# Sparse attention into a hard-swish MLP on one core: PSUM regrouped into four double banks, with score, value and GEMM 1 steps made wider

## The chip, the cores and the metric

The kernel runs on one core of a Trainium2 chip. The metric is the device time of one execution in microseconds (us), as the median of several runs; three runs of the kernel before gave 218.65 to 219.04 us with a median of 218.84 us. A core has five engines with a queue each: TensorE (PE, matmuls; its weight loads are listed as PEld), VectorE (DVE), ScalarE (ACT), GpSimd (POOL) and SyncE (SP). Here POOL and SP mostly issue DMAs. Matmuls write to PSUM, which has eight banks of 128 x 512 f32; DVE and ACT move results from PSUM to SBUF.

## The reference

Attention over 4 batches, 8 heads, 768 positions and head size 64, and then an MLP over the 3072 tokens. Each query sees the keys closer than 16 positions, plus 24 summary keys (the maximum of each block of 32 keys, with log 32 added to the score; the value is the mean of the block).

```
k_sum = k.reshape(B, H, nb, 32, D).max(3);  v_sum = v.reshape(B, H, nb, 32, D).mean(3)
scores_l = where(|i - j| < 16, q k^T / 8, -1e9);  scores_s = q k_sum^T / 8 + log(32)
attn = softmax(concat(scores_l, scores_s)) @ concat(v, v_sum)
x = attn.transpose(0, 2, 1, 3).reshape(3072, 512)
h = x @ w_in                                   # 512 -> 2048
out = (h * clip(h + 3, 0, 6) / 6) @ w_out      # 2048 -> 512
```

## The kernel before

**Attention.** A batch is cut into 12 blocks of 64 queries. A block meets 96 keys of its window and the 24 summary keys, so a score tile has 120 rows. Its plan names each step by a letter and numbers. `s` is the score step: matmuls of 64 x 64 for a pair of heads (`scores`, line 641), an `exp` on ACT that writes the tile `at` (line 651), and on DVE a product with a 0/1 mask (line 655). For batch 0 the first half of the queries instead gets its mask through a matmul with a bias (line 629). `u` forms the sums of the values (`vsum`, lines 665 and 682) and copies them into the tile `vaug`. `v` is the value step (`values`, line 742): at x vaug, with a column of ones that gives the softmax denominator, for tokens in tiles `T` of 128; `finish` takes the reciprocal (line 775), normalizes on DVE into `xn` (line 779) and turns it into `x` with tokens along the columns. For batches 0 and 1 the turn is four TensorE transposes (line 797) and a copy; for batches 2 and 3 it is a DMA transpose on SP's queue (line 789), one per `T`. `k`, `q` and `w` prepare transposed keys and queries; batch 0 and 1 do it with TensorE, batch 2 with DVE, batch 3 with DMA transposes (lines 570 and 579).

**The MLP.** A half batch of 384 tokens is a stage `s` (0 to 7). `F` is GEMM 1 (`f1`): for each of 16 blocks of 128 columns of w_in, four matmuls of 384 columns into one bank `h` (line 815), then a Relu on ACT into `r` (line 820) and min-and-multiply on DVE into `g` (line 822). `G` is GEMM 2 (`f2`): for each of the 3 token tiles, 16 matmuls of 512 columns into one bank, in four quarters of four (line 835), a copy to `ot` and a store by SP (lines 846 and 847).

**PSUM before.** Pools: three single banks `h` (GEMM 1), one single bank `o` (GEMM 2) and two double banks `S` (scores, values, transposes).

**Order.** The order of all steps is written out by hand in the long string `ORDER`; `F21.4` is step 4 of stage 2's second group of four column blocks, and a suffix `:A` or `:D` says that ACT or DVE does it. Each engine runs its own steps strictly in that order and waits on semaphores. `Plan.run` only picks buffers and adds a few filler matmuls on the tile `idle` (line 927) while PE waits in the first 23 us. Loads (`K`, `Q`, `V`, `h`, `I` for w_in, `O` for w_out) are issued by POOL in the same way; DMAs of x, keys and queries that transpose, and all stores, by SP.

Of the kernel before, what the change touches and what calls it, by code (L numbers as in the profile page):

```python
# [9 lines left out]
F32 = mybir.dt.float32  # L10
# [19 lines left out]
K01.0 K02.0 c.0 c.9 z1.0:D e.0 f.0 e.3 c.8 e.1 e.2 z0.0:A z2.0:A Q010.0 Q000.0 c.1 k01.0 k01.1 K00.0 k03.0 V00.0 c.2 c.4  # L30
k01.3:A z3.0:A k01.2:A k03.1 k02.0 s030.0 q030.0 q030.1:A q010.0 s010.0 k03.2:A q000.0 V02.0 V01.0 c.6 V03.0 k02.1 k02.3:A
k03.3:A k01.4 q010.1:D k02.4 k03.4 q000.1:D c.7 k02.2:D k00.0 s010.1 q020.0 s030.1 s010.2 q020.1:A s030.2 k00.1 k00.4 e.4
h000.0:D h020.0:D h010.0:D h021.0:D u00.0 s000.0 u00.1:A u00.2:A k00.2:A s020.0 s020.1 u02.0 s020.2 u01.0 s000.1 u01.1:A
s000.2 u02.1:A h011.0:D u01.2:D h030.0:D u03.0 u03.1:D h031.0:D v00.0 v02.0 v00.1 v01.0 v01.1 u01.3:A k00.3:A u02.2:A v00.2
v00.3 v02.2 v01.2 Q01w0.0 Q01w1.0 Q01w2.0 v02.1 v00.4 q021.0 q021.1:A s021.0 s021.1 v01.3 v00.5:D v02.3 v02.4 v02.5 I0.0 I1.0
I2.0 K11.0 c.3 I3.0 Q10.0 K10.0 K13.0 K15.0 K12.0 K14.0 Q13.0 Q14.0 Q11.0 Q15.0 Q12.0 O0.0 O1.0 O2.0 O3.0 h11.0 h10.0 q031.0
q031.1:A v02.6 v01.4 v01.5:A q011.0 q011.1:A u00.3:D v02.7:D u03.2:D c.5 h001.0:D F00.10 s031.0 s031.1 F00.0 F00.1 F00.2
F00.11 F00.12 q001.0 s031.2 F00.3 F00.13 q001.1:A F00.15 F00.16 F00.4 s021.2 F00.14 F00.17 s011.0 F01.0 s001.0 F01.9 F01.6
s011.1 F01.1 s011.2 F01.2 s001.1 s001.2 F01.10 F01.7 F01.11 F01.8 F00.5 F00.6 F00.7 v03.0 v04.0 F02.6 v03.1 v04.1 v03.2 F01.3
v04.2 v05.0 v03.3 F02.7 F00.8 F01.4 v03.4:A F02.8 v05.1 F00.9 v05.2 F01.5 F02.3 F02.4 F02.5 F02.0 v04.3 v05.3 F02.1 F02.2  # L40
v04.4:D v05.4:A F03.9 F03.3 F10.0 F03.10 F03.4 F10.1 F03.11 F03.5 F10.6 F13.9 F10.7 F13.10 F10.2 F10.8 F13.11 F03.6 F12.6
k10.0 F03.7 F03.8 k10.1:D k11.0 F12.7 F12.8 k11.1:D F10.9 k12.0 F10.10 F10.11 F02.9 F02.10 k12.1:A k13.0 F10.3 F03.0 F10.4
F02.11 k13.1:A F03.1 F10.5 F11.9 q11.0 F03.2 F11.10 q11.1:A F11.11 q10.0 F11.0 F11.3 q10.1:A F11.1 q13.0 q13.1:A F11.4 w1.0
F11.2 w1.4:D F11.5 G00.0 q12.0 F12.9 F12.0 F12.3 G00.1 F12.10 q12.1:A F12.1 w1.3:A G00.2 w1.1 w1.2:D s120.0 F12.2 F12.11
F11.6 G00.3 s120.3 s120.1 F13.0 s110.0 F11.7 F13.1 s110.1 s110.3 F12.4 G00.4:D F11.8 V13.0 V12.0 V10.0 V11.0 h12.0 G02.0
G02.1 s100.0 G02.2 G02.3 s100.1 s100.3 s130.0 F13.3 s130.1 s110.4 s110.2 F12.5 s120.4 G02.4:D G01.0 u1.0 G01.1 G01.2 s120.2
s100.2 s100.4 s130.2 F13.2 F13.4 s130.3 u1.1:A u1.4:A u1.8:D u1.6:D u1.2:D u1.7:A u1.5:A v10.0 G01.3 G01.4:A F13.6 u1.3:D
F13.5 v10.5 v10.1 v10.2 v10.6 s130.4 u1.9:D v10.3 v10.4:A F13.7 V21.0 K23.0 K20.0 K22.0 K21.0 V20.0 Q22.0 Q23.0 Q21.0 V23.0
Q20.0 h21.0 h20.0 K35.0 G11.0 G01.5 G02.5 G00.5 v12.0 F13.8 v12.5 v12.1 v12.2 v12.6 G11.1 G11.2 v10.7 v12.3 G11.3 v10.8:D
v12.4:D F20.0 F20.1 v12.7 v12.8:A F21.9 F21.6 F21.10 k21.0 k20.0 F21.7 F20.2 G11.4:D F21.11 F21.8 v14.0 F22.0 F20.9 F23.6  # L50
F20.10 F23.7 F22.1 k22.0 k23.0 F23.8 F22.2 v14.5 G12.0 G12.1 G12.2 F22.6 F22.7 F20.11 w2.0 v14.1 F22.8 v14.2 F21.0 F20.3
G12.3 F20.4 F21.1 F22.3 G12.4:A F22.4 F20.5 F21.2 v14.3 F20.6 F23.0 v14.6 F22.5 q20.0 F23.1 F20.7 v14.4:A w2.4:D F20.8 G10.0
v14.7 v14.8:A F22.9 G10.1 F21.3 F21.4 w2.3:A F22.10 G10.2 G10.3 w2.1 F23.2 F21.5 q22.0 F22.11 q21.0 F33.6 F30.0 G10.4:A F23.9
G20.0 G20.1 q23.0 q24.0:D w2.2:A F30.1 F30.2 F33.7 F33.8 F23.10 s210.0 F23.11 F32.9 F31.0 F23.3 s210.1 s210.3 F32.10 s220.0
s220.1 F31.1 F32.11 G20.2 F33.3 s220.3 F33.4 F23.4 F31.2 F33.5 F23.5 h31.0 V30.0 V32.0 h30.0 K34.0 V33.0 h22.0 V22.0 V31.0
h32.0 Q34.0 K30.0 Q31.0 u2.0 u3.0 u2.1:D u2.8:A u3.1:D u2.6:D F32.6 F30.6 F30.7 F33.9 s230.0 F33.10 u2.9:D F30.8 u2.2:D
F33.11 K32.0 K31.0 Q32.0 K33.0 Q33.0 Q35.0 Q30.0 G10.5 G12.5 k3e0.0 q3x0.0 G11.5 F32.7 s230.1 s230.3 G20.3 F31.6 F30.9 s200.0
G20.4:A u2.4:D s220.4 F32.8 u3.5:D s200.1 s210.2 s230.4 s200.2 s210.4 u2.5:D s220.2 s230.2 G21.0 F31.3 G21.1 G21.2 G21.3
u2.7:A s200.3 F31.7 F30.10 F31.8 F31.4 v20.0 F30.11 u2.3:D v20.1 F31.5 v20.4 G21.4:A v20.5 s200.4 v20.2 F31.9 F30.3 F31.10
F30.4 u3.8:A G22.0 G22.1 v22.0 F33.0 F33.1 G22.2 G22.3 G22.4:A v22.1 v22.4 F31.11 F30.5 F33.2 v22.2 v22.5 F32.3 F32.0 F32.1  # L60
F32.2 v24.0 F32.4 v24.4 F32.5 w3.0 w3.4:D v20.3 k3e1.0 v20.6 v22.3 G22.5 G30.0 G30.1 G30.2 G30.3 F40.0 F41.0 F43.9 G30.4:A
w3.1 F40.1 F41.1 F43.10 w3.2:D F40.2 w3.3:D v24.5 F41.2 u3.6:A F43.11 q3x1.0 G21.5 G30.5 v22.6 G20.5 v24.6 G32.0 G32.1 F40.6
F42.3 G32.2 F42.4 v24.1 v24.2 v24.3 F42.5 u3.9:A F40.7 F40.8 F43.3 F43.4 s320.0 F42.6 F42.0 s320.1 F42.7 s320.3 F42.1 F43.5
u3.7:D s320.2 F42.2 F41.6 F41.7 G32.3 G32.4:A s310.0 F42.8 F40.3 F40.4 u3.2:A F40.5 F50.0 F50.1 G31.0 F50.2 F41.8 u3.4:D
# [43 lines left out]
class Plan:  # L108
# [43 lines left out]

    def run(self):
# [7 lines left out]
        for token in ORDER.split():  # L161
# [8 lines left out]
            for a in o.alloc:  # L170
                a.pool = min((p for p in a.among if self.pools[p]), key=lambda p: min(x for x, _ in self.pools[p]))
                s = min(self.pools[a.pool], key=lambda s: s[0])
                self.pools[a.pool].remove(s)
                a.slot, t = s[1], max(t, s[0])
# [27 lines left out]
            for b in o.bufs:  # L202
                b.left -= 1
                b.used[e] = o.done
                b.end = max(b.end, o.done)
                if b.left == 0:
                    self.pools[b.pool].append((b.end + 0.02, b.slot))
                    self.lives.append((b.begin, b.end, b.slot))
# [761 lines left out]
```

## Time and profile before

| | |
|---|---|
| median of 3 runs | 218.84 us (218.65 to 219.04) |
| profiled execution, its own time | 219.68 us |
| its span in the profile | 217.9 us |
| granted TensorE clock | 0.999 |
| DVE busy | 148.3 us (68%) |
| ACT busy | 122.3 us (56%) |
| POOL busy | 71.2 us (33%) |
| DMA | 24.67 MB at a mean of 113 GB/s |

The profiled execution took 1.8 us more than its span, and 0.8 us more than the median of the runs. Busy time of an engine is not enough to say what bounds the kernel: matmuls are pipelined and their listed durations overlap, so the spacing of their starts, the chain of work that ended last and the waits have to be read beside it. The lines themselves are shown in the prediction.

### The profile page before, as it was taken

What the parts mean: (1) busy time and instruction counts of PE and PEld (TensorE: products, weight loads), DVE (VectorE), ACT (ScalarE), POOL (GpSimd) and SP (SyncE); (2) the same over time, 40 slices, a digit from 0 to 9 for tenths busy, and PEclk for the clock granted to TensorE, in tenths of its full rate; (3) what the DMA queues carried; (4) which work ended last, traced back from release to release, by engine and by line L of the source; (5) the groups of instructions that cost most, each with busy time, mean ns of one, the idle gap of its engine ahead of it and who ended that gap; (6) DMA issues with size and microseconds to landing.
All of it is one profiled execution on the core that took longest, in us unless ns stands there. A gap on an engine that the chain in (4) does not pass through costs nothing.

```text
span 217.9 us, 5201 instructions
## 1 busy us (share of the span) xinstructions
PE 207.1 (95%) x2125; PEld 118.4 (54%) x2151; DVE 148.3 (68%) x304; ACT 122.3 (56%) x236; POOL 71.2 (33%) x90
## 2 busy tenths in 40 slices
PE   7888999999989999989999999999999999999993
PEld 2566666765545555555555555555555555555552
DVE  4878998794898999849987866695555456333301
ACT  5697967797762545777742688833436343423010
POOL 7999369810988466296000000000000000000000
PEclk9999999999999999999999999999999999999999
DMA  5999999999999999999927920005421001201213
GB/s 68 182 156 191 201 164 159 205 195 147 122 120 164 169 122 143 162 172 148 212 52 180 230 26 0 3 0 157 135 48 51 0 2 50 99 0 48 86 59 100
DMA packets 109929, 24.67 MB, mean 113 GB/s; under 512 B 101072, under 2 KB 106960, under 8 KB 109904
## 3 DMA queue, kind: packets, MB, share of 16 engines
q0 software_dynamic: 93440, 14.89, 110.3%
q1 hardware_dynamic: 16464, 9.44, 16.4%
q8 instruction: 17, 0.28, 0.5%
q14 instruction: 8, 0.07, 0.1%
HBM read 29.77 MB, written 6.29 MB: 165 GB/s over the span
## 4 chain that ended last, share of the span: by engine, by line
PE 53%; DMA 25%; POOL 17%; issue 3%; ACT 0%; POOLq 0%; ACTq 0%
PE h L815 23%; PE o L835 22%; DMA vaug<-in_v_dram 20%; DMA win<-in_moe_w_in_dram 5%; PE h L835 5%; POOL nat L434 4%; POOL vaug L445 3%; POOL nat L425 2%; PE S L742 2%; POOL wout L485 1%; PE S L641 1%; POOL qwide L412 1%; POOL win L479 1%; POOL nat L392 1%; POOL nat L399 1%
## 5 line engine op out<-in xcount | busy, mean ns | idle before, releaser
L822 DVE SCALAR_TENSOR_TENSOR g<-r,h 128x384 bf16<-128x384 f32 x128 | 67.8, 547 | 42.6 <-ACT r L820 41.3
L815 PE MATMUL h<-x,win 128*128 128x384 bf16 (+1 forms) x536 | 94.5, 319 | 0.0
L820 ACT ACTIVATE r<-h 128x384 f32<-128x384 f32 x128 | 60.4, 496 | 55.2 <-PE h L815 51.6
L835 PE MATMUL o<-wout,g 128*128 128x512 bf16 x313 | 78.4, 379 | 1.6 <-issue 0.6
L815 PEld LDWEIGHTS <-win 128*128 128x128 bf16 x536 | 49.3, 98 | 34.0 <-issue 0.2
L835 PEld LDWEIGHTS <-g 128*128 128x128 bf16 x400 | 38.2, 98 | 37.2
L651 ACT ACTIVATE at<-S 120x768 bf16<-120x768 f32 x32 | 25.2, 816 | 4.7 <-PE S L641 4.6
L445 POOL DMA_DIRECT2D vaug<-in_v_dram x16 | 15.4, 968 | 4.4 <-DMA wout<-in_moe_w_out_dram 2.3
L655 DVE TENSOR_TENSOR at<-at,mask 96x768 bf16<-96x768 bf16 x28 | 14.7, 550 | 1.7 <-ACT at L651 1.6
L494 ACT COPY ot<-o 128x512 f32<-128x512 f32 x14 | 8.3, 589 | 13.3 <-PE o L835 13.2
L779 DVE TENSOR_TENSOR xn<-S,rc 128x512 bf16<-128x512 f32 x23 | 15.4, 683 | 0.3
L425 POOL DMA_DIRECT2D nat<-in_k_dram x12 | 10.7, 898 | 4.4 <-DMA win<-in_moe_w_in_dram 3.3
L425 POOL DMA_DIRECT2D nat<-in_q_dram x12 | 10.6, 897 | 1.9 <-DMA win<-in_moe_w_in_dram 1.9
L835 PE MATMUL h<-wout,g 128*128 128x256 bf16 (+1 forms) x64 | 10.7, 326 | 0.1
L707 DVE TENSOR_REDUCE red<-kb 128x48 bf16<-128x1536 bf16 x6 | 10.5, 1745 | 0.0
L641 PEld LDWEIGHTS <-kb 64*128 64x128 bf16 x384 | 6.8, 95 | 6.2 <-issue 5.0
L742 PEld LDWEIGHTS <-at 120*64 120x64 bf16 x360 | 6.7, 111 | 4.9 <-issue 2.9
L742 PE MATMUL S<-vaug,at 120*64 120x65 bf16 x352 | 8.0, 197 | 0.9 <-DVE vaug L494 0.9
L494 ACT COPY vaug<-vs 24x768 bf16<-24x768 bf16 x9 | 7.4, 828 | 1.1 <-DVE vs L494 0.9
L494 DVE COPY vaug<-vs 24x768 bf16<-24x768 bf16 x15 | 7.7, 517 | 0.5
L494 ACT COPY ot<-h 128x256 f32<-128x256 f32 (+1 forms) x3 | 1.3, 443 | 11.6 <-PE h L835 11.6
L494 DVE COPY ot<-o 128x512 f32<-128x512 f32 x7 | 4.8, 688 | 4.4 <-PE o L835 2.6
(107 smaller groups left out, 155.8 us busy)
## 6 DMA issues: line engine op xcount, KB each, us to landing
out_dram<-ot SPq DMA_DIRECT2D x19, 256.0 KB, 2.5
vaug<-in_v_dram POOLq DMA_DIRECT2D x16, 192.0 KB, 9.6
win<-in_moe_w_in_dram POOLq DMA_DIRECT2D x4, 512.0 KB, 9.4
wout<-in_moe_w_out_dram POOLq DMA_DIRECT2D x4, 512.0 KB, 10.0
nat<-in_k_dram POOLq DMA_DIRECT2D x12, 128.0 KB, 8.4
nat<-in_q_dram POOLq DMA_DIRECT2D x10, 128.0 KB, 5.4
nat<-in_k_dram POOLq DMA_DIRECT2D x6, 192.0 KB, 6.7
nat<-in_q_dram POOLq DMA_DIRECT2D x6, 192.0 KB, 10.7
```

The source lines that it names most:

```text
L425: nc.gpsimd.dma_start(out=o[n:128], in_=src[b, :, lo + n:lo + 128].rearrange("h r d -> r h d"))
L445: op("POOL", 0.945, lambda: nc.gpsimd.dma_start(out=o[BLK:WIN, lo:hi, 0:D], in_=rows[:, lo:hi]), w=[("v", b % 2, c)], dma=1.28, els=1536)
L494: {"ACT": nc.scalar.copy, "DVE": nc.vector.tensor_copy, "POOL": nc.gpsimd.tensor_copy}[eng](o, i)
L651: op("ACT", 0.81, lambda a=a, x=x: nc.scalar.activation(a, x.slot[0:KEYS, :, 0:HALF], AF.Exp, scale=scl), r=[x], w=[("at", p, half)])
L655: op("DVE", 0.55, lambda m=m, half=half: nc.vector.tensor_tensor(m, m, mask[:, low(half):low(half) + HQ].unsqueeze(1).to_broadcast([WIN, 2 ...
L707: nc.vector.tensor_reduce(red.slot[:].rearrange("x (p u e n) -> x e u p n", p=NP, u=NS, e=2)[:, e], w[:, n * e:n * e + n, BLK:WIN].rearran ...
L742: nc.tensor.matmul(y, a[:, cols], vaug[b % 2][0:KEYS, h, t, 0:D + 1], start=True, stop=True)
L779: nc.vector.tensor_tensor(o, src[..., 0:D], r.unsqueeze(len(r.shape)).to_broadcast(list(o.shape)), op=ALU.mult)
L815: nc.tensor.matmul(h.slot[:, lo * 128:hi * 128], w_in_sb[:, kt, ft * 128:(ft + 1) * 128], xt[s].slot[:, kt, lo * 128:hi * 128], start=(kt ...
L820: op("ACT", 0.49, lambda: nc.scalar.activation(r.slot[:], h.slot[:, 0:HALF], AF.Relu, bias=0.5, scale=1.0 / 6.0), r=[h], w=[r], alloc=r)
L822: op("DVE", 0.553, lambda: nc.vector.scalar_tensor_tensor(gt[s].slot[:, ft], r.slot[:], 1.0, h.slot[:, 0:HALF], op0=ALU.min, op1=ALU.mult) ...
L835: nc.tensor.matmul(o.slot[:, a:z], gt[s].slot[:, ft, ts * 128:(ts + 1) * 128], w_out_sb[:, ft, a:z], start=(ft == 0), stop=(ft == NFT - 1))
```

## The change

PSUM becomes two tiles of four banks. `S` is used as two double banks and `h` as four single banks or as two double banks (`hh`). Steps may take from either.

- **GEMM 1** does two column blocks at once into one double bank: the same matmuls, then one Relu and one min-and-multiply over 2 x 384 columns. `r` has two buffers of twice the size.
- **Scores** of batches 1 to 3: three steps (`scores_all`) of 32 matmuls, each into all four banks of `S`, with one `exp` over 2 x 1024 and one mask product, in place of four steps of 24 matmuls with two of each.
- **Values** of batches 1 to 3, and of the second half of batch 0: one step per half batch (`values_half`) of 48 matmuls into the four banks of `S`, one reciprocal and two normalizations, in place of one step per two tiles `T` (for batch 0: per tile).
- **x** of batches 1, 2 and 3: one DMA transpose per half batch. In batch 1 it takes the place of six groups of four TensorE transposes and their copies. Batch 0 still uses TensorE. `x` has three buffers in place of four.
- The constant tile `ind` is built on DVE, not on POOL; the constants `idle`, `band3`, `bias` and `sums` lie in the third `g` buffer.
- The last GEMM 2 tile is split into columns of 256, 128 and 128, not of 256 and 256.
- `ORDER` is new throughout. In the first stretch, batch 0's query block for the second half (`Q01w`) is loaded ahead of the values, and all of batch 0's scores and values come ahead of the first `F`.

```diff
-        "h": [ps.tile([128, 512], F32, tag=f"h{i}", name=f"h{i}") for i in range(3)],
-        "o": [ps.tile([128, 512], F32, tag="o0", name="o0")],
-        "S": pairs,
-        "x": [sb([128, NP, HALF], BF16, f"x{i}") for i in range(4)],
-        "r": [sb([128, HALF], F32, f"r{i}") for i in range(4)],
+    four = ps.tile([128, 4, 512], F32, tag="S", name="S")
+    banks = ps.tile([128, 4, 512], F32, tag="h", name="h")
+    pairs = [t[:, 2 * i:2 * i + 2] for t in (four, banks) for i in range(2)]
...
+        "h": [banks[:, i] for i in range(4)],
+        "S": pairs[:2],
+        "x": [sb([128, HALF // 128, NP, 128], BF16, f"x{i}") for i in range(3)],
+        "xm": [sb([128, 3 * d_model], BF16, "xm"), qwide[:].rearrange("p u m -> p (u m)")],
+        "r": [sb([128, 2, HALF], F32, f"r{i}") for i in range(2)],
...
+    def scores_all(b, k):
+        X, n = [Buf("S"), Buf("S")], NP * NQ // 3
...                                                   # 32 matmuls into four[:, 2 * j + i // 8, ...]
+        op("ACT", 1.88, lambda: nc.scalar.activation(odds[0:KEYS, :, w], four[0:KEYS].rearrange("p (j e) c -> p j (e c)", j=2), AF.Exp, scale=scl),
+           r=X, w=[("atg", k)])
+        op("DVE", 1.22, lambda: nc.vector.tensor_tensor(...mask..., op=ALU.mult), r=["mask", "masks"], w=[("atg", k)])
...
+    def values_half(b, half):
+        X, xm, rc, s, each = [Buf("S"), Buf("S")], Buf("xm"), Buf("rc"), 2 * b + half, 6
...                                                   # 48 matmuls into four[...]
+        op("DVE", 0.21, lambda: nc.vector.reciprocal(...), r=X, w=[rc], alloc=rc)
+        for g in range(2):
+            op("DVE", 0.97, lambda g=g: nc.vector.tensor_tensor(xm.slot[:, 768 * g:768 * g + 768]..., op=ALU.mult), ...)
+        if b:
+            op("SP", 1.3, lambda: nc.sync.dma_start(out=xt[s].slot[:].rearrange("p u k c -> p (u k) c"), in_=xm.slot[:], transpose=True), ...)
+            return
...                                                   # batch 0: TensorE transposes and copies
     def f1(s, ft):
-        h, r = Buf("h"), Buf("r")
+        h, r = Buf(("hh", "S")), Buf("r")
-        op("ACT", 0.49, lambda: nc.scalar.activation(r.slot[:], h.slot[:, 0:HALF], AF.Relu, bias=0.5, scale=1.0 / 6.0),
+        op("ACT", 0.81, lambda: nc.scalar.activation(r.slot[:], h.slot[:, :, 0:HALF], AF.Relu, bias=0.5, scale=1.0 / 6.0),
-        op("DVE", 0.553, lambda: nc.vector.scalar_tensor_tensor(gt[s].slot[:, ft], r.slot[:], 1.0, h.slot[:, 0:HALF],
+        op("DVE", 0.955, lambda: nc.vector.scalar_tensor_tensor(gt[s].slot[:, ft:ft + 2], r.slot[:], 1.0, h.slot[:, :, 0:HALF],
...
-        for p in range(NP):
-            scores(b, [(p, 0), (p, 1)])
+        for i in range(3):
+            scores_all(b, i)
         vsum(b)
-        for Ts in ((0, 1), (2, 3), (4, 5)):
-            values(b, Ts)
+        for x in range(2):
+            values_half(b, x)
...
-                f2(s, *part, cols=(0, d_model // 2))
-                f2(s, *part, cols=(d_model // 2, d_model))
+                for c in ((0, 256), (256, 384), (384, 512)):
+                    f2(s, *part, cols=c)
```

The parts of the new `ORDER` that the prediction speaks of: the end of the start, the last part of batch 1's attention with GEMM 1 of stages 3 and 2, and the end.

```
... u02.0 u02.1:A u02.2:A h011.0:A u01.3:A ... v00.0 v01.0 v00.1 v01.1 v02.0 v02.1 ... v00.4 v01.3 v03.0 ...
v02.2 v02.3 v00.5:A v01.4 v01.5:D v03.1 v02.4 v03.2 v03.3 F00.0 F00.1 F00.2 ...
... v13.0 v13.1 v13.2 v13.3 G00.5 v13.4 G01.5 G12.0 G02.1 G02.2 v10.0 G12.1 G12.2 G02.3 G12.3 k22.0
v10.1 v10.2 k21.0 v10.3 k23.0 G12.4:A G12.5 G11.5 F30.0 F30.1 F30.4 F30.5 F31.0 F31.1 ... F33.3 v10.4 G02.5 F20.0 ...
... G62.0 G62.1 G62.2 G62.3 G72.4:D G72.5 G71.1 G71.4 G71.7 G71.12 G62.4:A G62.5 G71.13:A G71.14
```

More of the change, by code (lines that the diff above doesn't have):

```diff
@@ L43 @@
[L43 to L52, printed above, removed]
@@ L85 @@
 SLOW = 5.8
+TAKEN = 1e9
 TURN = 0.11
@@ L151, in room, with take, give @@
         return t
+    def take(self, a):
+        best = None
+        for p in a.among:
+            own = self.pools["h" if p == "hh" else p]
+            ts = [max(own[2 * m:2 * m + 2]) for m in range(len(own) // 2)] if p == "hh" else own
+            for n, x in enumerate(ts):
+                if x < TAKEN and (best is None or x < best[0]):
+                    best = x, p, n
+        t, a.pool, n = best
+        a.at = [("h", 2 * n), ("h", 2 * n + 1)] if a.pool == "hh" else [(a.pool, n)]
+        for p, m in a.at:
+            self.pools[p][m] = TAKEN
+        a.slot = self.slots[a.pool][n] if a.pool != "hh" else self.wide[n]
+        return t
+    def give(self, a):
+        for p, m in a.at:
+            self.pools[p][m] = a.end + 0.02
+            self.lives.append((a.begin, a.end, self.slots[p][m]))
     def run(self):
@@ L170, in run @@
             for a in o.alloc:
[L171 to L174, printed above, removed]
+                t = max(t, self.take(a))
             for k in o.bufs:
@@ L276 @@
     qwide = sb([128, NS // 2, d_model], BF16, "qwide")
-    sums = sb([128, NP, 2, D + 2], BF16, "sums")
-    vf = [sums[:, c] for c in range(NP)]
     w_in_sb = sb([128, NP, d_ff], BF16, "win")
@@ L301 @@
     })
+    plan.wide = pairs[2:]
     op = plan.op
@@ L346, in const_ops @@
         op("DVE", 0.64, over=0.0, fn=spread, r=["band", "band3"], w=["mask"])
+        op(EITHER, {"ACT": 0.85, "DVE": 0.45}, lambda eng: copy(eng, mask[:, NQ:2 * NQ], mask[:, 0:NQ]), r=["mask"], w=["masks"])
         def blocks():
-            nc.gpsimd.memset(ind[:], 1.0)
-            nc.gpsimd.affine_select(out=ind[:], in_=ind[:], compare_op=ALU.is_ge, fill=0.0, base=-BLK, channel_multiplier=1,
-                                    pattern=[[QB, NQ], [-BLK, 32]])
-            nc.gpsimd.affine_select(out=ind[:], in_=ind[:], compare_op=ALU.is_ge, fill=0.0, base=2 * BLK - 1, channel_multiplier=-1,
-                                    pattern=[[-QB, NQ], [BLK, 32]])
-        op("POOL", 1.74, blocks, w=["ind"])
-        op("DVE", 0.22, lambda: nc.vector.memset(ind[0:BLK], 0.0), w=["ind"])
+            nc.vector.memset(ind[:].bitcast(F32), 0.0)
+            flat = ind[:].rearrange("p t n -> p (t n)")
+            for lo, at in ((BLK, 0), (QB, 1)):
+                nc.vector.memset(flat[lo:lo + BLK, at::34], 1.0)
+        op("DVE", 0.45, over=0.03, fn=blocks, r=["idle"], w=["ind"])
         def edges(i):
@@ L874 @@
             halo(0, p, x)
-    for T, banks in enumerate((None, None, ("h", "h"))):
-        values(0, (T,), banks=banks, by_pair=True)
+    for T in range(3):
+        values(0, (T,), by_pair=True)
     for p in range(NP):
@@ L879 @@
         scores(0, [(p, 1)])
-    for T in (3, 4, 5):
-        values(0, (T,))
+    values_half(0, 1)
     for b in range(1, B):
@@ L929 @@
     order = plan.run()
-    banks = [s for p in BANKS for _, s in plan.pools[p]]
+    rooms = [x for p in ("S", "h") for x in plan.slots[p]]
     todo, end = [], BEGIN["PE"]
@@ L934 @@
             n = int(max(min(o.begin, SLOW) - end, 0.0) / 0.43 + max(o.begin - 0.15 - max(end, SLOW), 0.0) / 0.22) + (end == BEGIN["PE"])
-            idle_ = [s for s in banks if not any(a < o.begin and z > end and x is s for a, z, x in plan.lives)]
+            idle_ = [s for s in rooms if not any(a < o.begin and z > end and x is s for a, z, x in plan.lives)]
             if n > 0 and idle_:
```

206 lines of the change are left out of this document (127 added, 79 removed).

## The prediction

> **What bounds the kernel now.** I read the page's busy shares first, then busy time by stretch, the chain of work that ended last, the timeline of TensorE and the waits. Columns of the second view: stretch and length in us, busy us and instructions of each engine, granted clock, DMA share, GB/s.
>
> ```profile
> PE 207.1 (95%) x2125; PEld 118.4 (54%) x2151; DVE 148.3 (68%) x304; ACT 122.3 (56%) x236; POOL 71.2 (33%) x90
> ```
>
> ```profile
> 0.00:23.00 23.00, 19.02 (x322) 12.01 (x326) 17.18 (x49) 16.80 (x35) 20.92 (x36) 1.00 1.47 152
> 70.00:90.00 20.00, 19.89 (x147) 11.24 (x147) 19.10 (x31) 11.66 (x25) 11.08 (x13) 1.00 3.48 149
> 104.00:204.00 100.00, 99.31 (x781) 53.57 (x792) 61.31 (x124) 49.03 (x96) 0.00 (x0) 1.00 0.29 70
> ```
>
> TensorE is busy for 95% of the span, at full clock. From 104 to 204 us it is busy 99.31 of 100 us, while DVE works 61 and ACT 49: there only fewer microseconds of matmul, or of gaps between kinds of matmul, can help. From 70 to 90 us DVE is nearly full too (19.10 of 20). The first 23 us differ: TensorE is listed as busy, but much of that is filler, and ACT works 16.80 of 23.
>
> The chain gives what a step costs on TensorE (start, us, what, how many):
>
> ```profile
> 111.09 0.63 PE S L742 x32
> ...
> 126.18 0.46 PE S L641 x24
> 126.64 2.06 PE h L815 x12
> 131.42 1.73 PE o L835 x8
> 133.15 1.95 PE h L815 x12
> ```
>
> Twelve GEMM 1 matmuls take 1.95 us (0.163 each, 0.65 for a set of four), four of GEMM 2 take 0.865. After a score or value step the same pieces are 0.11 longer (2.06 for twelve): a switch costs that on top of 0.46 for 24 score or 0.63 for 32 value matmuls.
>
> **The change, part by part.** The sum is made in time on TensorE, against the span of 217.9 us; the profiled execution took 219.68 us, 0.84 above the median of 218.84, and I take the same difference off both.
>
> *GEMM 1 two banks at a time.*
>
> ```profile
> L822 DVE SCALAR_TENSOR_TENSOR g<-r,h 128x384 bf16<-128x384 f32 x128 | 67.8, 547 | 42.6 <-ACT r L820 41.3
> L820 ACT ACTIVATE r<-h 128x384 f32<-128x384 f32 x128 | 60.4, 496 | 55.2 <-PE h L815 51.6
> L651 ACT ACTIVATE at<-S 120x768 bf16<-120x768 f32 x32 | 25.2, 816 | 4.7 <-PE S L641 4.6
> L779 DVE TENSOR_TENSOR xn<-S,rc 128x512 bf16<-128x512 f32 x23 | 15.4, 683 | 0.3
> ```
>
> The matmuls stay. 128 Relus of 0.496 become 64 of about 0.82 (the `exp` of 768 columns takes 0.816); 128 DVE steps of 0.547 become 64 of about 0.95 (from 683 ns at 512 columns and 547 at 384, 1.06 ns a column). ACT saves 64 x (0.99 - 0.82) = 11 us, DVE 64 x (1.09 - 0.95) = 9. Both wait for others most of the time (41.3 and 51.6 us before these very steps), so I cost the saving at 0. The cover is that a pair takes TensorE 1.30 us and DVE 0.95; the price if it goes is a rival below.
>
> The Trainium skill's page "Perfetto Trace Analysis" (Optimizing Scalar/DVE Operations) says larger operations improve throughput when the engine is saturated, but where Scalar and Vector are not and cause bubbles elsewhere, breaking instructions up lets work finish sooner. By it this part would be a loss of the rival's size; the shares of 68% and 56% fit its second case, and 19.10 of 20 us its first.
>
> *Fewer switches, in batches 1 to 3.* Scores: 24 matmuls cost 0.46 + 0.11 = 0.57. A set of 12 cost 0.38 at the start (timeline below: 0.28 and a gap of 0.10), so 0.0158 a matmul and 0.19 a step; 32 cost 0.70. Nine of 0.70 for twelve of 0.57: -0.5. Values: 32 cost 0.74, 16 cost 0.48 (0.38 and 0.10), 48 then 1.00. Six of 1.00 for nine of 0.74: -0.7. Together -1.2.
>
> *The start, and what moves ahead of it.* The timeline of TensorE around the first GEMM 1 matmul:
>
> ```profile
> 22.96 0.39 PE L815 MATMUL h<-x,win 128*128 128x128 bf16 x4
> ...
> 23.56 1.29 PE L815 MATMUL h<-x,win 128*128 128x128 bf16 x20
> 24.69 0.33 PE L561 MATMUL S<-ident,qwide 128*128 128x128 bf16 x3
> 24.85 0.81 PE L815 MATMUL h<-x,win 128*128 128x384 bf16 x4
> 25.60 0.35 PE L641 MATMUL S<-q,kb 64*128 64x64 bf16 x12
> 25.88 0.82 PE L815 MATMUL h<-x,win 128*128 128x384 bf16 x4
> ...
> 28.99 0.70 PE L742 MATMUL S<-vaug,at 120*64 120x65 bf16 x32
> 29.62 1.47 PE L815 MATMUL h<-x,win 128*128 128x384 bf16 x8
> 31.02 0.44 PE L742 MATMUL S<-vaug,at 120*64 120x65 bf16 x16
> 31.40 0.40 PE L797 MATMUL S<-ident,xn 128*128 128x128 bf16 x4
> 31.63 1.46 PE L815 MATMUL h<-x,win 128*128 128x384 bf16 x8
> ```
>
> GEMM 1 begins at 22.96; from there TensorE is the bound. In the new order three score steps of batch 0's second half (0.38 each, 1.14), one transposition of queries (0.16) and its values (0.73 + 0.48) run before the first GEMM 1 matmul, in time that TensorE spends waiting: -2.5 behind the start.
>
> Against it the start moves. Ahead of the first copy of x on ACT:
>
> ```profile
> 7.15 0.76 ACT L494 COPY kb<-h 128x480 bf16<-128x480 bf16 x3 [3.47 <-DVE red L530]
> 22.99 0.58 ACT L494 COPY x<-o 128x512 bf16<-128x512 bf16 x1
> ```
>
> ```profile
> L494 ACT COPY kb<-h 128x480 bf16<-128x480 bf16 (+3 forms) x15 | 4.8, 406 | 3.5 <-DVE red L530 3.5
> ```
>
> By the two instruction orders ACT now has eight `exp` ahead of that copy in place of five (3 x 0.816 = +2.4 us), one more copy of q (+0.5), one of the sums (+0.3), a halo copy of about 1.0, and four key copies fewer (4 x 0.406 = -1.6): +2.6. After 7.15 us it is nearly gapless until 22.99, so little can slip in; successive ACT instructions overlap slightly. The values also land later, behind `qwide`. I take +2.0 (bounds 0.5, if gaps absorb it, and 3.5, if the later values add to it): GEMM 1 at about 25.0.
>
> *x of batch 1 by DMA.* Six groups of four transposes go: 31.63 - 31.40 = 0.23 each, -1.4 on TensorE. Six copies leave ACT and DVE, hidden anyway. The price is latency. In the new order both GEMMs of stages 0 and 1 are used up when `F30.0` comes: between the value step `v13.0` and it lie seven quarters of GEMM 2 (7 x 0.865) and the value step `v10.0` (1.00), 7.05 us. In that time DVE takes the reciprocal and two normalizations of 768 columns (0.2 + 2 x 0.95 = 2.1), so 4.9 us are left for the DMA. Rows for it: first the large transposes of batch 3's queries, later, with little other traffic; then stores and loads in the middle of the load stream, which is where the new transposes fall.
>
> ```profile
> L570 SPq DMA_TRANSPOSE qb<-nat x2: 1456/1722/1987, 104.7 to 117.9; - x2
> DMA to landing us min/median/max: 3.2/3.7/4.1
> ```
>
> ```profile
> L847 SPq DMA_DIRECT2D out_dram<-ot x3: 403/411/733, 65.2 to 66.1; - x3
> DMA to landing us min/median/max: 6.9/7.4/7.6
> ```
>
> ```profile
> nat<-in_q_dram POOLq DMA_DIRECT2D x4, 192.0 KB, 11.3
> ```
>
> Quiet, 3.7 us: no stall. Among loads, a DMA from the same SP queue took 7.4: a stall of 2.5. Behind all loads queued before it, 11.3 and then its own 3.7, 15.0: a stall of 10.1. I take 7.4, the same queue in the same phase: +2.5. Behind the waiting `F30.0` everything on TensorE waits, as its queue is in order. The second half's x has ten sets of GEMM 1 (6.5 us) more before `F20.0`, and I cost it at 0. On SP only stores stand beside these DMAs. In batches 2 and 3, with the loads over, two large transposes in place of six small ones have 7 us and more in the new order: 0.
>
> *Two stalls that go.*
>
> ```profile
> PE S L742 <- DVE vaug L494: 0.9, 1, 0.9
> PE S L682 <- DMA vaug<-in_v_dram: 0.6, 1, 0.6
> ```
>
> The only long waits of TensorE after 23 us: batch 1's first value step for copied sums, and a sum for a load. In the new order more work stands ahead of both: -1.5. The next to come late is x, costed above.
>
> *The end.*
>
> ```profile
> 213.96 0.99 SPq L847 DMA_DIRECT2D out_dram<-ot  x2
> 214.21 0.37 ACT L494 COPY ot<-h 128x256 f32<-128x256 f32 x1 [1.85 <-PE h L835]
> ```
>
> The last copy has 128 columns, not 256 (about 0.27 for 0.37), and the last store half the bytes: -0.25 (bounds 0 and -0.4). The split costs no time on TensorE: twenty matmuls of 128 columns took 1.13 us (23.56 to 24.69), 0.056 each against 0.109 for 256. The Trainium skill's "TensorE: Matmul & The Clock Gate" (Back-to-back issue gap) gives 81 ns for 128 columns in a real stream of loads and matmuls; by it the 32 narrow ones would add 0.8 us. The trace has 56 ns, and the trace decides.
>
> *`ind` on DVE, constants in a shared buffer, three buffers of x.* All inside the waits of the start or far from their next use: 0.
>
> Sum: +2.0 - 2.5 - 1.4 - 1.2 - 1.5 + 2.5 - 0.25 = -2.35. The span becomes 215.55, the median 218.84 - 2.35 = 216.5 us.
>
> **Rivals.**
>
> *x is in time* (no stall at `F30.0`): 216.5 - 2.5 = 214.0. For it: 3.7 us where the queue was quiet, and loads may pause while POOL waits for the value buffer. Against it: 7.4 in that phase. [...] Chance 0.22.
>
> *x is late* (slower). The transpose lands behind all loads in the queue: 15.0 for 7.4, 216.5 + 7.6 = 224.1. It turns the sign once issue to landing exceeds 4.9 + 4.85 = 9.75 us, 4.85 being the gain without a stall. For it: 11.3 us of loads in that window. Against it: the stores' 7.4. Chance 0.13.
>
> *Wide steps starve TensorE* (slower). A score step keeps four of eight banks for 0.61 us of matmul and about 1.88 of `exp` (816 ns plus 1280 columns at 0.83, from 816 and 496), a value step for 2.1 of DVE. GEMM 1 then has two pairs with a round of 1.30 + 0.82 + 0.95 = 3.1 us for 2.6 us of matmul: 0.5 idle a round where no GEMM 2 quarter stands between. One such round at each of 15 wide steps is 7 us: 216.5 + 7 = 223.5, half of them 220. Against it: the new order puts quarters between nearly all of them. Chance 0.12, a third of it still faster.
>
> *The start eats it.* GEMM 1 two more microseconds late: 218.5 to 219, no change. For it: ACT's chain; against it: ACT has 1.7 us of idle time there. Chance 0.07.
>
> *Forecast:* 0.46, at 216.5; its own range 214.5 to 218.
>
> **How the numbers follow.** Faster by over 0.2% (some 0.4 us, about what a measurement can tell from no change): 0.46 + 0.22 + 0.04 = 0.72. Same: 0.05, from the start's case. Slower: 0.13 + 0.08 + 0.02 = 0.23. The range goes down to 212.5 (no stall, start only 0.5 later) and up to 220.8, which leaves out the late x and the worst of the starving.
>
> **What would show it.** Right: the first GEMM 1 matmul near 25.0; a wait of TensorE at GEMM 1's first matmul on stage 3 of 1 to 4 us, put down to the DMA of x; large transposes at 70 to 80 us with 6 to 9 us to landing; no waits for PSUM in 104 to 204 us; last matmul near 212. Wrong: GEMM 1 after 27; that wait absent or above 5 us; many waits of TensorE on DVE or ACT before GEMM 1, each of some 0.3 us or more.

## The result, and the profile after

The changed kernel takes 306.94 us (median of four runs, 305.55 to 307.35) against 218.75 for the kernel before in the same series (218.12 to 219.04): a ratio of 1.402, 95% interval 1.3973 to 1.4068. It is 88 us slower, where 216.5 was forecast and 220.8 was the upper end. The profiled execution took 306.94 us, with a span of 305.2. Ratios here and below leave disturbed runs out, which the medians do not.

The page of the changed kernel: busy times with their share of the span, the clock granted to TensorE in 40 slices of 7.6 us (in tenths, 9 is 90% or more), and the lines of the chain that ended last.

```profile
PE 229.7 (75%) x2153; PEld 126.6 (41%) x2153; DVE 142.6 (47%) x210; ACT 111.2 (36%) x147; POOL 69.6 (23%) x87
PEclk9655556999999999978999999999999999999999
PE h L909 28%; PE S L887 10%; PE h L887 10%; DVE g L895 10%; ACT r L893 7%; DMA x<-xm 5%; PE h L1000 3%; DVE ot L505 2%; PE h L702 2%; ACT ot L505 2%; PE S L807 2%; ACT kb L505 2%; DVE red L541 1%; DVE kb L505 1%; PE h L520 1%
```

No engine became the bound: DVE and ACT have fewer busy microseconds than before (148.3 and 122.3) in a span 87 us longer. Before, almost the whole chain after 97 us was TensorE. Now the min-and-multiply (L895) and the Relu (L893) stand in it with 17%, beside GEMM 1 (L887) and GEMM 2 (L909): the engines take turns. By stretch, with the columns of the prediction's second view:

```profile
0.00:23.00 23.00, 12.32 (x115) 5.82 (x115) 9.21 (x27) 8.22 (x16) 19.35 (x33) 0.72 1.50 152
23.00:51.50 28.50, 20.81 (x299) 15.19 (x300) 12.60 (x34) 12.44 (x22) 18.94 (x21) 0.51 1.86 180
104.00:204.00 100.00, 77.15 (x757) 40.38 (x757) 56.08 (x72) 38.43 (x47) 22.84 (x26) 0.97 0.97 102
```

Between 104 and 204 us TensorE stands still for 22.9 us in 100; it was 0.7. The other part is the start, where it is busy for 12.32 of 23 us and then gets half the clock. Its timeline (start, us, what, how many; in brackets the idle time before and what ended it):

```profile
13.03 1.01 PE L1000 MATMUL h<-g 128*128 128x512 bf16 x2 [2.91 <-DVE red L541]
17.21 1.44 PE L1000 MATMUL h<-g 128*128 128x512 bf16 x3 [2.71 <-ACT kb L505]
51.48 0.38 PE L887 MATMUL h<-x,win 128*128 128x128 bf16 x4 [0.52 <-DVE x L505]
...
255.50 0.81 ACT L893 ACTIVATE r<-S 128x768 f32<-128x768 f32 x1 [0.55 <-PE S L887]
256.36 0.81 PE L887 MATMUL S<-x,win 128*128 128x384 bf16 x4 [0.96 <-ACT r L893]
257.01 2.76 PE L887 MATMUL h<-x,win 128*128 128x384 bf16 x16
257.21 0.81 ACT L893 ACTIVATE r<-S 128x768 f32<-128x768 f32 x1 [0.90 <-PE S L887]
258.05 1.82 DVE L895 SCALAR_TENSOR_TENSOR g<-r,S 128x768 bf16<-128x768 f32 x2 [2.12 <-ACT r L893]
259.81 1.51 ACT L893 ACTIVATE r<-h 128x768 f32<-128x768 f32 x2 [1.79 <-PE h L887]
```

GEMM 1 starts at 51.48 us (before: 22.96). L1000 is the filler, constants into a bank that nobody uses. It is there so that TensorE does not idle, and yet it waits 2.91 us for DVE, which is reading *another* bank of `h`. The second group shows the same inside the MLP. At 255.50 ACT reads the first pair of `S`; the next matmul into `S` starts right behind it, at 256.36, though it writes to the other pair (the first pair is still needed by DVE at 258.05). From 257.01 TensorE fills both pairs of `h` with 16 matmuls, and ACT, idle, starts on the first of them only when all 16 have ended. (Part of this wait may be for `r`, whose first buffer DVE gives back near 259.0.) Some waits of the whole execution (us in total, times, longest):

```profile
ACT r L893 <- PE S L887: 40.6, 18, 5.6
...
DVE g L895 <- PE S L887: 22.8, 10, 5.1
ACT r L893 <- DVE g L895: 22.2, 14, 2.3
...
PE S L887 <- DVE g L895: 9.2, 10, 1.6
...
PE S L887 <- ACT r L893: 7.4, 8, 1.4
```

ACT waits for DVE (22.2 us, before 2.5) and DVE directly for TensorE (22.8), both odd: a Relu needs nothing from a min-and-multiply but a free `r` (which now has two buffers), and a min-and-multiply comes after its Relu. I read one cause in this, **theory A**: an instruction on one bank waits for the other engines' work on all banks of the same PSUM *tile*, and the change put eight banks into two tiles where there had been six. Its rivals were **B**, the wide steps hold too many banks, and **C**, the new order is bad by itself; later **D** to **J** for what was left.

### The profile page after: what moved, and what is told of

Same layout as the page of the kernel before. It is cut to its first block, busy times and chain, and to the rows that moved or that the text cites. A ratio compares the mean times of both kernels' runs of the same rounds, so it can differ in the third digit from the quotient of the medians.

```text
span 305.2 us, 5005 instructions
## 1 busy us (share of the span) xinstructions
PE 229.7 (75%) x2153; PEld 126.6 (41%) x2153; DVE 142.6 (47%) x210; ACT 111.2 (36%) x147; POOL 69.6 (23%) x87
## 3 DMA queue, kind: packets, MB, share of 16 engines
q1 hardware_dynamic: 19488, 10.23, 14.3%
## 4 chain that ended last, share of the span: by engine, by line
PE 61%; DVE 16%; ACT 14%; DMA 5%; issue 3%; DVEq 0%; ACTq 0%
PE h L909 28%; PE S L887 10%; PE h L887 10%; DVE g L895 10%; ACT r L893 7%; DMA x<-xm 5%; PE h L1000 3%; DVE ot L505 2%; PE h L702 2%; ACT ot L505 2%; PE S L807 2%; ACT kb L505 2%; DVE red L541 1%; DVE kb L505 1%; PE h L520 1%
## 5 line engine op out<-in xcount | busy, mean ns | idle before, releaser
L909 PE MATMUL h<-wout,g 128*128 128x512 bf16 (+2 forms) x416 | 90.5, 362 | 19.1 <-DVE ot L505 5.1
L887 PEld LDWEIGHTS <-win 128*128 128x128 bf16 x544 | 51.9, 99 | 75.1 <-issue 39.7
L887 PE MATMUL S<-x,win 128*128 128x384 bf16 (+1 forms) x312 | 55.3, 318 | 16.7 <-DVE g L895 9.2
L909 PEld LDWEIGHTS <-g 128*128 128x128 bf16 x416 | 38.5, 97 | 62.4 <-issue 24.4
L887 PE MATMUL h<-x,win 128*128 128x384 bf16 (+1 forms) x232 | 42.9, 328 | 18.2 <-DMA x<-xm 5.5
L895 DVE SCALAR_TENSOR_TENSOR g<-r,S 128x768 bf16<-128x768 f32 x37 | 34.9, 953 | 37.8 <-PE S L887 22.8
L893 ACT ACTIVATE r<-S 128x768 f32<-128x768 f32 x37 | 29.8, 810 | 54.8 <-PE S L887 40.6
L895 DVE SCALAR_TENSOR_TENSOR g<-r,h 128x768 bf16<-128x768 f32 x27 | 25.6, 953 | 30.0 <-ACT r L893 18.0
L893 ACT ACTIVATE r<-h 128x768 f32<-128x768 f32 x27 | 21.8, 810 | 35.0 <-PE h L887 20.9
L456 POOL DMA_DIRECT2D vaug<-in_v_dram x16 | 15.2, 958 | 50.9 <-PE S L807 48.7
L689 ACT ACTIVATE at<-S 120x2048 bf16<-120x2048 f32 x9 | 16.9, 1877 | 18.4 <-PE S L683 18.4
L1000 PE MATMUL h<-g 128*128 128x512 bf16 x21 | 9.9, 611 | 10.7 <-DVE red L541 3.5
L691 DVE TENSOR_TENSOR at<-at,mask 96x2048 bf16<-96x2048 bf16 x9 | 10.6, 1218 | 8.3 <-ACT at L689 8.3
L1000 PEld LDWEIGHTS <-g 128*128 128x128 bf16 x21 | 2.4, 125 | 13.1 <-issue 8.5
```

The costliest lines, as they stand in the source:

```text
L456: op("POOL", 0.945, lambda: nc.gpsimd.dma_start(out=o[BLK:WIN, lo:hi, 0:D], in_=rows[:, lo:hi]), w=[("v", b % 2, c)], dma=1.28, els=1536)
L689: op("ACT", 1.88, lambda: nc.scalar.activation(odds[0:KEYS, :, w], four[0:KEYS].rearrange("p (j e) c -> p j (e c)", j=2), AF.Exp, scale=sc ...
L691: op("DVE", 1.22, lambda: nc.vector.tensor_tensor(odds[0:WIN, :, w].rearrange("p j (t c) -> p j t c", c=QB), odds[0:WIN, :, w].rearrange(" ...
L887: nc.tensor.matmul(h.slot[:, f, lo * 128:hi * 128].rearrange("p (u c) -> p u c", c=128), w_in_sb[:, kt, (ft + f) * 128:(ft + f + 1) * 128] ...
L893: op("ACT", 0.81, lambda: nc.scalar.activation(r.slot[:], h.slot[:, :, 0:HALF], AF.Relu, bias=0.5, scale=1.0 / 6.0), r=[h], w=[r], alloc=r)
L895: op("DVE", 0.955, lambda: nc.vector.scalar_tensor_tensor(gt[s].slot[:, ft:ft + 2], r.slot[:], 1.0, h.slot[:, :, 0:HALF], op0=ALU.min, op1 ...
```

## The experiments

Differences between kernels are worked out below as differences of the ratios to the kernel before, times 218.75 us.

**e1 and e2: one of the two tiles cut into two.** Only the declaration of `h` changes in e1, no instruction. In e2 `S` is cut, and the `exp` and the reciprocal over four banks become two each.

```diff
-    banks = ps.tile([128, 4, 512], F32, tag="h", name="h")
+    hp = [ps.tile([128, 2, 512], F32, tag=f"h{i}", name=f"h{i}") for i in range(2)]
-        "h": [banks[:, i] for i in range(4)],
+        "h": [hp[i // 2][:, i % 2] for i in range(4)],
...                                                            # e2:
-    four = ps.tile([128, 4, 512], F32, tag="S", name="S")
+    fs = [ps.tile([128, 2, 512], F32, tag=f"S{i}", name=f"S{i}") for i in range(2)]
-        ... nc.scalar.activation(odds[0:KEYS, :, w], four[0:KEYS]..., AF.Exp, scale=scl),
+        ... [nc.scalar.activation(odds[0:KEYS, j, w], fs[j][0:KEYS]..., AF.Exp, scale=scl) for j in range(2)],
```

> The changed kernel (306.9 us) with its tile h of four banks made into two tiles of two banks; S stays one tile of four. Nothing else changes. Theory A (shared tiles: an instruction on one bank of a PSUM tile waits for the other engines' work on all banks of that tile, so GEMM 1, the Relu, min-and-multiply and GEMM 2 run one after another instead of side by side): the waits at h inside the MLP mostly go, those at S stay; 235 to 280 us, with the first GEMM 1 matmul before 45 us in place of 51.5. Theory B (wide steps hold too many banks, so GEMM 1 starves): 300 to 308, as the banks in use are the same. Theory C (the new order of steps is bad by itself): 300 to 308.

> The changed kernel with its tile S made into two tiles of two banks; h stays one tile of four. The exp and the reciprocal, which read four banks at once, become two instructions of two banks each (costs some 0.2 us for each of nine exps). Theory A: the waits at S go, those at h stay; 250 to 300 us, a smaller gain than with h split, since G and most of GEMM 1 use h. Theories B and C: 303 to 310.

Measured, two runs each: e1 263.0 us, e2 294.6 (ratios 1.202 and 1.346). GEMM 1 began at 36.2 us in e1 and 50.7 in e2. Both are as A expects. Since e1 has the instructions of the changed kernel, in their order and of their sizes, B and C have no place for its 44 us. The waits follow the cut. DVE's min-and-multiplies in e1 (`h` cut), then in e2 (`S` cut; "..." stands for other lines of the page):

```profile
L895 DVE SCALAR_TENSOR_TENSOR g<-r,S 128x768 bf16<-128x768 f32 x37 | 34.9, 952 | 44.2 <-PE S L887 24.7
...
L895 DVE SCALAR_TENSOR_TENSOR g<-r,h 128x768 bf16<-128x768 f32 x27 | 25.6, 951 | 10.5 <-ACT r L893 10.1
```

```profile
L895 DVE SCALAR_TENSOR_TENSOR g<-r,h 128x768 bf16<-128x768 f32 x27 | 25.6, 953 | 38.8 <-ACT r L893 23.0
L895 DVE SCALAR_TENSOR_TENSOR g<-r,S 128x768 bf16<-128x768 f32 x37 | 34.8, 951 | 15.6 <-ACT r L893 15.3
```

In the changed kernel DVE was idle for 37.8 us before its steps on `S` and for 30.0 before those on `h`; only the tile that is cut improves. The same settles a rival, that two buffers of `r` are too few: they stay two, and yet ACT's wait for DVE goes from 14.1 to 1.8 us at the Relus from `S` in e2, and from 8.1 to 1.1 at those from `h` in e1.

**e3: both tiles cut.** The edits of e1 and e2 together, four tiles of two banks.

> The changed kernel with both PSUM tiles made into two tiles of two banks, in the same order of steps and with the same wide steps. Theory A: 213 to 228 us, no loss against the kernel before beyond a few us, first GEMM 1 matmul at 24 to 30 us, clock granted at full from about 10 us on. Theory B: 290 us or more, with waits of TensorE at h and S as many as in the changed kernel. Theory C: 290 us or more. A result between 230 and 290 would leave part of the loss to B or C.

Measured: 240.3 us (1.087; 1.0808 to 1.0929). Three quarters of the loss are gone (0.315 of 0.402), but A's 213 to 228 was missed, and by what was expected a result between 230 and 290 leaves part of the loss to B or C. The profiled execution took 242.5 us, 2.2 above the median, so its rows serve for places, not for sums. TensorE:

```profile
37.76 2.55 PE L887 MATMUL h<-x,win 128*128 128x128 bf16 x22
...
105.11 4.73 PE L887 MATMUL h<-x,win 128*128 128x384 bf16 x16 [7.33 <-DMA x<-xm]
```

The start is still 15 us late, and the wait for x (5.5 us in the changed kernel) is 7.33.

**e4 and e8: the mirror.** The kernel before, in its old order and with its narrow steps, gets merged tiles: e4 one of four banks for `h` and `o` and one for `S`; e8 two tiles of two for `h` and `o`, `S` untouched.

```diff
-        "h": [ps.tile([128, 512], F32, tag=f"h{i}", name=f"h{i}") for i in range(3)],
-        "o": [ps.tile([128, 512], F32, tag="o0", name="o0")],
+        "h": [singles[:, i] for i in range(3)],        # e4: singles = ps.tile([128, 4, 512], ...)
+        "o": [singles[:, 3]],                           # e8: hp[i // 2][:, i % 2], hp = two tiles [128, 2, 512]
-    pairs = [ps.tile([128, 2, 512], F32, tag=f"S{i}", name=f"S{i}") for i in range(2)]
+    pairs = [doubles[:, 2 * i:2 * i + 2] for i in range(2)]   # e4 alone; doubles = ps.tile([128, 4, 512], ...)
```

> The kernel before (218.8 us) with nothing changed but the PSUM tiles: its four single banks h and o become slices of one tile of four banks, its two double banks S slices of another. Order, steps, sizes and buffers as before. Theory A: 270 to 330 us, as each single bank now waits for the three others. Theories B and C: 218 to 219.5, as no step is wider and the order is the old one.

> The kernel before (218.8 us) with its four single banks put in two tiles of two (two banks for GEMM 1 together, the third with that of GEMM 2); S and all else as before. Theory A: between 218.8 and the 463.4 us of the fully merged kernel, at 240 to 340 us: GEMM 1's banks wait for each other in pairs, and GEMM 2 for one of GEMM 1. Theories B to F: 218 to 219.5.

Measured, two runs each: e4 463.4 us, e8 278.0 (ratios 2.117 and 1.270). The tuned kernel's time doubles by the declarations of its PSUM tiles alone. Its waits in e4 (line numbers are two higher than before):

```profile
DVE g L824 <- ACT r L822: 95.5, 43, 8.4
ACT r L822 <- PE h L817: 94.5, 37, 7.6
ACT r L822 <- DVE g L824: 55.1, 32, 4.0
PE h L817 <- DVE g L824: 52.9, 46, 2.2
```

For e4 I had expected 270 to 330; e8 lies within its 240 to 340. The old order suffers more than the new one. A likely reason, not tested, is that a round of turns there carries one bank of GEMM 1 and not two.

**e5, e6 and e7: what e3 left.** In e5 the four banks of `h` become four tiles of one bank; a step that uses two of them does its Relu, min-and-multiply, `exp` or normalization in two instructions (`S` stays in tiles of two). In e6, on e3, x of batch 1 is turned by TensorE as in batch 0. e7 is both.

```diff
-    banks = ps.tile([128, 4, 512], F32, tag="h", name="h")                  # e5, e7
+    hs = [ps.tile([128, 512], F32, tag=f"h{i}", name=f"h{i}") for i in range(4)]
...
-        op("ACT", 0.81, lambda: nc.scalar.activation(r.slot[:], h.slot[:, :, 0:HALF], AF.Relu, ...),
+        op("ACT", 0.81, lambda: [nc.scalar.activation(r.slot[:, f], h.slot[:, f, 0:HALF], AF.Relu, ...) for f in range(2)]
+           if isinstance(h.slot, Two) else nc.scalar.activation(r.slot[:], h.slot[:, :, 0:HALF], AF.Relu, ...),
...
-        if b:                                   # e6, e7: values_half, x by one DMA transpose
+        if b > 1:
...                                             # ORDER: v13.4 to v13.9 stand behind G02.2, v10.4 to v10.9 behind k23.0
```

> The kernel with both PSUM tiles split (240.3 us, first GEMM 1 matmul at 37.8, a stall of 7.3 us on the DMA of x at 98 to 105 us), with one more step: the four banks of h become four tiles of one bank. A step that uses two banks of h then does its Relu, min-and-multiply, exp or normalization in two instructions of one bank. Theory A (sharing of a tile): the start was still late because the two single banks of a pair wait for each other; first GEMM 1 matmul at 24 to 29 us, clock at full in the start, 226 to 233 us; the stall on x stays. Rival D (the new order itself makes the start late, as it puts another load and more ACT work ahead): first GEMM 1 matmul stays after 34 us, 236 to 243.

> The kernel with both PSUM tiles split into pairs (240.3 us), with x of batch 1 turned by TensorE and copied by ACT and DVE, as in batch 0, in place of the two DMA transposes. Theory E (the DMA of x, 12.2 us to landing among the value loads, is the only cause of the 7.3 us stall): the stall goes, 24 transposes and their switches come back at 1.4 us; 233 to 236 us. Rival F (another load or a sum is just as late, so the wait only moves to the next step): 238 to 242.

> Both at once: h as four tiles of one bank, and x of batch 1 turned by TensorE. Theories A and E: the two gains add up; 218 to 227 us. If D or F holds instead: 230 us or more.

Measured: e5 224.8 us (1.0175; 1.0091 to 1.0259), e6 232.5 (1.0628; 1.0579 to 1.0677), e7 217.93 (0.9949; 0.9913 to 0.9984). The gains add up: from e3, 15.2 us for single tiles (1.0869 - 1.0175), 5.3 for x in time, 20.1 together. All three medians lie just below the low end of what was expected. e5 is the change as it was drawn, without shared tiles where it uses single banks. Its TensorE, SP and POOL (L898 is GEMM 1, L827 the transpose of x, L464 the value loads, L932 stores):

```profile
25.04 2.88 PE L898 MATMUL h<-x,win 128*128 128x128 bf16 x32
...
71.65 0.94 POOL L464 DMA_DIRECT2D vaug<-in_v_dram  x1 [4.47 <-PE S L815]
...
71.88 4.66 SPq L932 DMA_DIRECT2D out_dram<-ot  x3
...
75.19 2.77 PE L898 MATMUL S<-x,win 128*128 128x384 bf16 x16 [0.17 <-DMA x<-qwide]
76.64 2.95 SPq L827 DMA_TRANSPOSE x<-xm  x1
...
78.55 1.88 POOL L464 DMA_DIRECT2D vaug<-in_v_dram  x2
...
87.65 4.13 PE L898 MATMUL h<-x,win 128*128 128x384 bf16 x16 [5.78 <-DMA x<-xm]
```

D falls: the start is at 25.04 us as soon as single banks are single tiles. E holds: the second transpose of batch 1, issued at 76.64, lands 11.0 us later, and TensorE stands 5.78 us for it. POOL had waited for the value buffer, which the value step L815 frees at 71 us; so its loads go out together with the very transpose that follows from that step. SP's queue adds to it: the transpose's input is ready at 74.45 (DVE's last normalization starts at 73.53 and takes 0.92), but three stores hold the queue until 76.54. That the loads and not the stores make the 11.0 us is likely and not tested alone: in e9 a transpose of batch 2 went out at 124.24, with three stores in the 4 us before it and no loads, and landed in 3.2 us.

**e9 and e10: a version that keeps what paid.** e9 is e5 with only the first half of batch 1 (`v10`, the late one) turned by TensorE. e10 also evacuates GEMM 1 in `S` one bank at a time, so that nothing of the wide evacuation is left.

```diff
-        if b:                                   # e9
+        if b > 1 or b and half:
...                                             # ORDER: the six steps v10.4 to v10.9 stand behind k23.0
-        ... if isinstance(h.slot, Two) else nc.scalar.activation(r.slot[:], h.slot[:, :, 0:HALF], AF.Relu, ...)    # e10, and
+        ... [nc.scalar.activation(r.slot[:, f], h.slot[:, f, 0:HALF], AF.Relu, ...) for f in range(2)]             # L868 so too
```

> As the kernel with h in four tiles of one bank and x of batch 1 turned by TensorE (217.9 us), but only the first half of batch 1 is turned by TensorE (its DMA transpose took 11.0 us to landing among the value loads, and TensorE stood 5.8 us for it); the second half goes back to its DMA transpose, for which TensorE waited 0.2 us. 12 transposes and three switches go (0.23 x 3 = 0.7 us). Theory A with E (late only where the value loads are ahead): 216.5 to 218, no wait on x over 0.5 us. Rival F (the second half only came in time because the first half held TensorE up later): 218 to 220, with a wait for x before stage 3.

> The kernel of e9 with one more edit: GEMM 1 in the double banks of S is evacuated one bank at a time too (two Relus and two min-and-multiplies of 384 columns in place of one of 768). 37 pairs of steps; by durations 0.50 x 2 for 0.81 on ACT and 0.55 x 2 for 0.95 on DVE: 7 us more of ACT, 5 us more of DVE in all. Theory H (evacuation lies behind other engines' work, so its width is worth nothing): within 0.7 us of e9. Rival I (wide evacuation is what makes the new order work): 2 us or more slower than e9, with waits of TensorE on DVE in GEMM 1.

Measured: e9 217.65 us (0.9921; 0.9888 to 0.9953); e10 217.58 (0.9936; 0.9909 to 0.9964). The intervals of e7, e9 and e10 overlap, so none of the three is shown to be the fastest. e9 and e10 are 0.3 us apart, so H holds; F does not, as e9 is below its 218. No wait for x is left over 0.29 us. In e9 the 100 us read:

```profile
104.00:204.00 100.00, 98.68 (x973) 55.61 (x985) 59.59 (x93) 48.56 (x73) 0.00 (x0) 1.00 0.25 67
```

GEMM 1's evacuation from `S` in e10, beside which e9 and the changed kernel have 37 steps of 951 and 811 ns:

```profile
L868 DVE SCALAR_TENSOR_TENSOR g<-r,S 128x384 bf16<-128x384 f32 x74 | 37.1, 548 | 18.6 <-ACT r L866 18.6
L866 ACT ACTIVATE r<-S 128x384 f32<-128x384 f32 x74 | 32.1, 490 | 27.8 <-PE S L860 27.1
```

**e11: the filler.** e9 without the filler matmuls.

```diff
-            if n > 0 and idle_:
+            if False:
                 todo.append(lambda n=n, s=idle_[-1]: keep(n, s))
```

> The kernel of e9 without the filler matmuls on constants in the first 25 us. This asks how much of the late start of the changed kernel may be the granted clock alone. Theory J (an idle TensorE is granted half the clock, as in the first 50 us of the changed kernel): clock 0.5 to 0.8 in the first 30 us, first GEMM 1 matmul 1 to 5 us later than in e9, 2 to 8 us slower in all. Rival (the low clock there was only a companion of the waits): within 1 us of e9.

Measured: 220.13 us (1.0061; 1.0037 to 1.0086), 3.1 us more than e9 by the ratios; GEMM 1 starts at 28.30 us, in e9 at 26.29. Both are as J expects. So the filler is worth 2 to 3 us, and its absence alone explains little of the 28.5 us by which GEMM 1 came later in the changed kernel than before. The timeline of e9, then that of e11, then the first 23 us of e11 in the columns of the windows:

```profile
7.14 0.87 PE L490 MATMUL h<-ident,nat 96*64 96x96 bf16 x32
26.29 2.83 PE L860 MATMUL h<-x,win 128*128 128x128 bf16 x32
```

```profile
7.99 1.49 PE L490 MATMUL h<-ident,nat 96*64 96x96 bf16 x32 [0.57 <-DMA nat<-in_k_dram]
28.30 2.83 PE L860 MATMUL h<-x,win 128*128 128x128 bf16 x32
```

```profile
0.00:23.00 23.00, 14.82 (x263) 11.04 (x265) 17.82 (x49) 16.62 (x37) 19.52 (x33) 1.00 1.48 151
```

J's clock of 0.5 to 0.8 is not in the clock column of e11 (1.00), but the 32 transposes took 1.49 us for 0.87, and until 18 us a set of twelve score matmuls took 0.50 for 0.35: there the durations have to be read, not the column.

**The sum.** By ratios: 1.402 to 1.0869 by cutting the tiles of four (69 us), to 1.0175 by single tiles (15), to 0.9921 by turning one half on TensorE (6). So shared tiles cost 84 us and the late x 6, and a gain of 2 us (1.0 to 2.4 by its interval) lay underneath: 84 + 6 - 2 = 88. Cut alone, `h` brought 44 us and `S` 12, cut together 69, so the two do not simply add. e9 keeps the wide score and value steps, and the new order but for the six steps, without loss: nothing is left for B and C.

## Why the prediction was wrong

**What bounds the kernel** was read rightly: TensorE, with DVE and ACT waiting. It did not say what made that possible. The kernel before shows no wait for a neighbouring bank, because none of its tiles holds banks that different steps use side by side.

**GEMM 1 two banks at a time** is the step that failed: "I cost the saving at 0. The cover is that a pair takes TensorE 1.30 us and DVE 0.95". The durations were right (0.82 and 0.95 forecast; 810 and 953 ns in the changed kernel), and so was the 0 for the width (e10). But the cover assumed that pairs run side by side. The diff showed `ps.tile([128, 4, 512])`, and the prediction priced the banks and not the tiles: 84 us that no term and no rival held. In place of the cover the changed kernel shows waits: ACT for DVE 22.2 us (before 2.5), and TensorE idle for 22.9 us of the 100.

**The start** was put at +2.0 with GEMM 1 at about 25.0. With single tiles it is 25.04 in e5, and 25.72 to 27.05 in e10, e9 and e7, which have the same start. So ACT's longer chain was sized about right, at the low end. In the changed kernel it is 51.48: transposes, copies and the filler wait for each other in `h`, and then TensorE works at half the clock. Of the 20.81 us that it is busy between 23 and 51.5, full clock would save at most 20.81 x (1 - 0.51) = 10 us, an estimate from that row.

**x of batch 1 by DMA** was sized too low and put in the wrong place: +2.5 at `F30.0` with 7.4 us to landing, and 0 for the other half. In e5 `F30.0` waits 0.17 us (its transpose went out just before the value loads and landed in 4.8) and `F20.0` 5.78, with 11.0 to landing. The rival "x is late" had a wait of this kind, but at `F30.0`; its bound of 9.75 us belongs to that place. e5, at 1.0175, is slower than the kernel before, so even without the sharing among the single banks the forecast would have had the wrong sign. The step behind it: "ten sets of GEMM 1 (6.5 us) more before `F20.0`" counted the cover, but neither the 2 us behind SP's stores nor what the freed value buffer sets off on POOL. Among loads such a transpose took 11.0 us, in batches 2 and 3 of e9 3.2 to 3.3.

**Switches, transposes, work moved ahead, stalls gone, end** can be judged only as a sum. Without the stall 214.0 was forecast, and 0.7 for the 12 transposes of e9 gives 214.7; e9 stands at 0.9921 x 218.84 = 217.1, 2.4 us more. Its GEMM 1 starts 1.3 us later than 25.0; the granted clock there was 0.50 from 23 to 26 us, and the value step of 48 matmuls took 1.53 us, where e10 at a clock of 1.00 took 0.95. In 104 to 204 us TensorE is busy 98.68, not 99.31 (0.6 us). The last 0.5 us is not located. That e9 comes so near to the 216.5 of the forecast is luck, as the forecast held a stall of 2.5 us that e9 does not have.

**The rival "wide steps starve TensorE"** had the sign and the place, not the mechanism: e9 has the same wide score and value steps and no such idle time (98.68 of 100 us busy). **"What would show it"** named the right sign of failure (GEMM 1 after 27 us, many waits before GEMM 1), without a cause for it. The sums of the prediction come out as they are stated; only its upper end, 220.8, is not worked out there.

## What to carry to other kernels

When a change regroups buffers, ask first what the unit of waiting is: here it was the tile as declared, not the bank, and its declaration alone took the tuned kernel from 218.9 to 463.4 us. Declare one PSUM tile for each group that is written and read as one, and merge only as far as a single instruction really spans; a filler that waits, or an engine that starts on the first buffer only when the second is full, is the sign in a trace. For a DMA that has to land in time, look at what the same event lets loose on the other queues.

## What the runs showed of the hardware

- A DMA transpose of 128 x 1536 took 3.2 to 3.3 us to landing after the loads were over (e9; one of four in e5 5.2), but 11.0 (e5), 12.2 (e3) and 14.3 us (changed kernel) when value loads and three stores were issued in about 5 us before it.
- After TensorE's idle 5.8 us in e5 the granted clock was 0.80 from 88 to 94 us and 1.00 after that; in the changed kernel's start, with waits of up to 2.6 us one after another, it was 0.51 over 28.5 us. The Trainium skill's "TensorE: Matmul & The Clock Gate" (What's actually happening) says that the default is throttled and activity releases it; the two rows agree with it. How much idle time it takes they do not say: in e9 the clock fell to 0.50 from 23 to 26 us after a stretch (18 to 23 us) in which TensorE was busy 4.09 of 5 us, in e10 it stayed at 1.00 after 4.22 of 5.
- Evacuating 768 columns in one instruction saved no time of the kernel against two of 384, on engines that wait for TensorE anyway (e9 and e10, 0.9921 and 0.9936).
